# A list scheduler that counts VectorE's hold on GpSimd, first conversions ranked later, the guard moved into layer two, and a fourth silu buffer

## The chip, the cores and the metric

The kernel runs on one core of one Trainium2 chip. The metric is device microseconds of one execution, as the median of several runs. A core has a matrix engine (PE, TensorE), a vector engine (DVE, VectorE), an activation engine (ACT, ScalarE), a general engine (POOL, GpSimd), and a queue engine (SP, SyncE) that issues most of the DMAs. Each engine executes its own instructions strictly in the order in which they were written; engines wait for one another through semaphores.

## The reference, cut to what matters

A recurrent attention with 4 x 8 heads over 768 time steps, its output reshaped to 3072 tokens of 320 numbers, and then two dense layers on them:

```python
for t in range(S):                       # state: 40x40 for each of 32 heads
    y[:, :, t] = einsum('bhd,bhde->bhe', rt, state)
    Sa = einsum('bhde,bhe->bhd', state, at)
    state = state * wt[:, :, None, :] - einsum('bhd,bhe->bhde', Sa, bt) + einsum('bhd,bhe->bhde', vt, kt)
...
h = x @ w_in;  g = h * sigmoid(1.702 * h);  x = g @ w_out          # layer one, 320 -> 2048 -> 320
g = x @ w_gate;  x = (silu(g) * (x @ w_val)) @ w_out2              # layer two, 320 -> 1536 -> 320
```

The inputs are float32, but the weights of both layers arrive as float64, two 32-bit words to a number.

## The kernel before

**Attention.** The 768 time steps are cut into 12 pieces of 64 ("steps" from here on), which are solved one after the other for all heads at once. In a step VectorE scans the decays (L629, L648), k, b and a are scaled by them (L654 for kb, L658 for a, on VectorE or GpSimd), PE multiplies them (L680, L884), VectorE solves a triangular system in a long row of small products and updates (L760/L768 in the first five steps, L704/L712 later), PE and ScalarE join the parts (L802 to L854), and w, u, the state and y follow (L925 to L1100). Two steps give one block of 512 tokens, of which there are six.

**Layer one.** A block of 512 tokens goes through 16 slices of 128 hidden units: eight matmuls into the one PSUM bank h (L448), a silu on ScalarE into one of the buffers sg (L456), a high part gh (L462), a low part gl (L463), and eight matmuls into acc (L475 to L482) two slices later. After a block's sixteen slices three more sg buffers take its output (L494, L497, L504), from which DMAs write it to x2s in DRAM (L500, L508). There are three sg buffers; a silu waits until the DMA that reads its buffer has landed.

**Weights.** A weight piece (rows x 256 numbers) is loaded as float64 (L268, buffers cva) and turned into float32 by integer operations: L283 and L288 on VectorE, L280 on ScalarE, L296 on GpSimd. Beside it runs a guard, which finds numbers too small for this conversion. For the 44 pieces of layer one it is two ScalarE instructions (L271 squares, L274 compares and sums into flags); for the 45 pieces of layer two it is a minimum on VectorE (L299, into least). At the very end a flag is made of them (L1195 to L1206).

**What sets the order.** The attention and layer one are recorded as tasks with an engine (or two to choose from, VectorE or GpSimd), a cost and a due time, and a list scheduler (Plan.order) puts them into the order in which they are written. It knows that VectorE and GpSimd exclude each other (the variable port). Where it expects PE to be idle it writes filler matmuls on zeros (L408, tile still). Layer one's tasks have the last due time, so that they fill gaps of the attention. For tasks due before SOON, PE may wait up to 2 us for one that is due earlier. The tasks whose start is planned after the last attention task (the tail) are written one by one, with eleven small jobs of layer two's conversion after each slice. Layer two then runs in program order: for each of six blocks and twelve slices f sixteen matmuls (L1353), silu, product, high and low part (L1357 to L1360), and twelve matmuls of an earlier slice (L1372 to L1374).

Of the kernel before, what the change touches and what calls it, by code (L numbers as in the profile page):

```python
# [6 lines left out]
F32 = mybir.dt.float32  # L7
# [23 lines left out]
C_G = 192  # L31
# [40 lines left out]
class Plan:  # L72
# [6 lines left out]
    NEAR, SOON = {"PE": 2.0}, 2.5  # L79
# [40 lines left out]
    def order(self):  # L120
# [14 lines left out]
        def start(t, e):  # L135
# [90 lines left out]
class Convert:  # L226
# [4 lines left out]
    def __init__(self, tc, ctx, cst=None, flags=None):  # L231
        self.tc, self.nc = tc, tc.nc
        self.cst, self.flags = cst, flags
# [4 lines left out]
        self.count = self.parts = 0  # L238

# [7 lines left out]
    def piece(self, src, finish, least=None):  # L247
# [25 lines left out]
        def small():  # L273
            nc.scalar.activation(  # L274
                out=w, in_=w, func=ACTF.Relu, scale=-1.0, bias=self.cst[0:rows, C_G + 5:C_G + 6],
                accum_out=self.flags[0:rows, i:i + 1],
            )

# [19 lines left out]
        def smallest():  # L298
            v.tensor_reduce(  # L299
                out=least[0:rows], in_=hi.bitcast(F32), axis=AXL.X, op=ALU.min, apply_absolute_value=True  # L300
            )
# [7 lines left out]
        return [("SP", 0.5, load, (), (ak, ak + "l"), rows * cw / 128)] + check + [  # L309
            ("DVE", 0.25, shift, (ak,), (uk,), 0),  # L310
            ("DVE", 0.46, join, (ak,), (uk,), 0),
            guard,
            ("ACT", 0.44, low, (), (ak + "l",), 0),
            ("POOL", 0.78, add, (uk, ak + "l"), (wk,), 0),
        ] + finish(w)

# [26 lines left out]
class Up:  # L343
# [9 lines left out]
    def __init__(self, tc, ctx, keep, cst, w_out, x2s, side):  # L353
# [8 lines left out]
        self.sg = [k.tile([128, n], F32, name=f"sg{i}") for i in range(3)]  # L362
# [4 lines left out]
        self.still = k.tile([128, n], F32R, name="still")  # L367
# [38 lines left out]
    def warm(self):  # L406
        c = self.still
        self.nc.tensor.matmul(self.ph[0], c[:, 0:128], c, start=True, stop=True)  # L408

    def tasks(self, plan):  # L410
# [14 lines left out]
        def sg_slot():  # L425
            self.nsg += 1
            return (self.nsg - 1) % 3
# [763 lines left out]
def bad_flag(nc, tc, down, cst, flags, least, good, bad):  # L1191

    with tc.tile_pool(name="fl2", bufs=1, side="right") as p:
        m = p.tile([128, 1], F32, name="fl_f")
        nc.vector.tensor_reduce(out=m, in_=flags, axis=AXL.X, op=ALU.max)  # L1195
        nc.vector.tensor_scalar(out=m, in0=m, scalar1=0.0, scalar2=None, op0=ALU.is_le)
        nc.vector.tensor_tensor(m, m, good, op=ALU.mult)
        n = p.tile([128, 1], F32, name="fl_l")
        nc.vector.tensor_reduce(out=n, in_=least, axis=AXL.X, op=ALU.min)
        nc.vector.tensor_scalar(out=n, in0=n, scalar1=TINY, scalar2=None, op0=ALU.is_ge)  # L1200
        nc.vector.tensor_tensor(m, m, n, op=ALU.mult)
# [7 lines left out]
def layer_one(att, up, conv, jobs):  # L1209
# [26 lines left out]
class Down:  # L1236
# [5 lines left out]
    def __init__(self, tc, ctx, cst, conv, weights, x2s, out, up, least):  # L1242
# [8 lines left out]
        self.up, self.lag, self.n = up, [], 0  # L1251
        self.jobs = self.convert(conv, *weights)

# [5 lines left out]
    def convert(self, conv, gv, gv_rest, out, out_rest):  # L1259
# [46 lines left out]
        loads, makes, ends, n = [], [], [], 0  # L1306
        for f, src, fin in todo:
            got = []
            steps = conv.piece(src, lambda w: got.append(w) or [], self.least[:, n:n + 1])
            n += 1  # L1310
# [34 lines left out]
    def h_part(self, m, f):  # L1345
# [9 lines left out]
        sg, hi, lo = (t[self.n % 3] for t in (self.up.sg, self.up.gh, self.up.gl))  # L1355
# [28 lines left out]
    def prepare(self, n=0, f=-1):  # L1384

        while self.jobs and (n > 0 or self.jobs[0][0] <= f):
            self.jobs.pop(0)[1]()
            n -= 1
# [6 lines left out]
    def run(self):  # L1395
        for m in range(NSTEP):
            parts = iter(())
            for f in range(NF2):
# [9 lines left out]
                next(parts, None)  # L1408
                self.prepare(8)
# [7 lines left out]
def general(tc, cst, seq, w_in, w_out, w_gate, w_val, w_out2, xn, out):  # L1417
# [7 lines left out]
    with ExitStack() as ctx:  # L1425
# [64 lines left out]
        with ExitStack() as cx:  # L1490
            conv = Convert(tc, cx)

# [235 lines left out]
```

## Time and profile before

| | us |
|---|---|
| median of 3 runs (lowest to highest) | 1160.1 (1158.8 to 1166.8) |
| the profiled execution, its own time | 1152.7 |
| its span | 1150.9 |
| PE busy | 1103.5 (96%) |
| DVE busy | 683.8 (59%) |
| ACT busy | 474.6 (41%) |
| POOL busy | 165.1 (14%) |

The page says which engine carries the end: PE, with the fillers counted as busy. So the share of PE alone does not tell where time can go; the stretches, with the granted clock in each, and the waits of PE in them do. A filler is busy time that computes nothing, and a PE row at the lower clock takes twice as long as it has to.

### The profile page before, as it was taken

The page shows a single profiled execution, that of the slowest core. Times are in us where ns is not written, and L with a number is a line of the kernel's source. Part 1 is how long each engine was busy: PE and PEld are TensorE (multiplying, and loading weights), DVE is VectorE, ACT ScalarE, POOL GpSimd, SP SyncE. Part 2 cuts the span into 40 slices and gives each one's busy share as a digit, 9 for nine tenths or more (in the row PEclk, how much of TensorE's full clock was granted, in tenths as well). Part 3 has the DMA queues.
Part 4 walks back from the last instruction along what each step waited for, and adds up shares of the span by engine and source line. Part 5 has one row for each costly group of instructions (what it writes and reads, how often), then busy time and mean ns, then how long its engine had stood idle before and what let it go on. Part 6 is the DMA issues. An engine that isn't in the chain of part 4 may idle for free.

```text
span 1150.9 us, 39910 instructions
## 1 busy us (share of the span) xinstructions
PE 1103.5 (96%) x17425; PEld 914.1 (79%) x17425; DVE 683.8 (59%) x1400; ACT 474.6 (41%) x941; POOL 165.1 (14%) x144
## 2 busy tenths in 40 slices
PE   9888899989999999889999998999999999999996
PEld 7676777777887888768888786888888888888886
DVE  6856858686785959495876376878323232332222
ACT  3456577753434334333335355644222222222221
POOL 2222224250102002002110032322000000000000
PEclk9888999989999999998999999999999999999999
DMA  6245456553534444242423356733100101010000
GB/s 215 82 130 179 147 159 203 162 159 106 187 97 128 147 132 141 72 153 72 156 81 94 104 178 193 213 106 103 51 1 13 39 1 51 1 51 1 24 1 26
DMA packets 116440, 119.68 MB, mean 104 GB/s; under 512 B 13216, under 2 KB 107168, under 8 KB 116256
## 3 DMA queue, kind: packets, MB, share of 16 engines
q1 hardware_dynamic: 111288, 110.16, 31.4%
q10 hardware_dynamic: 4968, 6.88, 1.7%
q8 instruction: 138, 2.26, 0.8%
q14 instruction: 46, 0.38, 0.1%
HBM read 95.76 MB, written 13.11 MB: 95 GB/s over the span
## 4 chain that ended last, share of the span: by engine, by line
PE 84%; DVE 8%; issue 3%; DMA 2%; SPq 1%; ACT 1%; ACTq 0%; DVEq 0%
PE gv L1353 23%; PE h L448 14%; PE acc L480 4%; PE oacc L1374 4%; PE oacc L1373 4%; PE oacc L1372 4%; PE acc L482 3%; PE acc L481 3%; PE h L408 3%; PE ps L1120 2%; PE ps L1070 2%; PE ps L994 2%; PE acc L476 2%; PE acc L475 2%; DVE tmp L704 1%
## 5 line engine op out<-in xcount | busy, mean ns | idle before, releaser
L1353 PE MATMUL gv<-xst,wg 128*128 128x512 f32 x1152 | 274.4, 390 | 0.0
L1353 PEld LDWEIGHTS gv<-xst,wg 128*128 128x128 f32 x1152 | 213.5, 188 | 41.2
L448 PE MATMUL h<-xst,wi 120*128 120x512 f32 x768 | 202.0, 405 | 3.5 <-ACT sg L456 2.8
L448 PEld LDWEIGHTS h<-xst,wi 120*128 120x128 f32 x768 | 141.9, 190 | 37.5 <-ACT sg L456 3.4
L1358 DVE TENSOR_TENSOR sg<-gv,sg 128x512 f32<-128x512 f32 x72 | 49.7, 690 | 194.7 <-PE gv L1353 194.7
L456 ACT ACTIVATE sg<-h 128x512 f32<-128x512 f32 x96 | 57.2, 596 | 169.5 <-PE h L448 152.5
L296 POOL TENSOR_TENSOR cvw<-cvu,cva 128x256 uint32<-128x256 uint32 (+2 forms) x89 | 83.4, 938 | 264.9 <-DVE cvu L288 124.0
L463 DVE TENSOR_TENSOR gl<-sg,gh 128x512 fp32r<-128x512 f32 x81 | 59.0, 729 | 82.1 <-ACT gh L462 81.9
L1359 ACT ACTIVATE gh<-sg 128x512 fp32r<-128x512 f32 x72 | 45.5, 632 | 137.2 <-DVE sg L1358 137.2
L1357 ACT ACTIVATE sg<-gv 128x512 f32<-128x512 f32 x72 | 42.8, 595 | 128.5 <-PE gv L1353 128.5
L1374 PE MATMUL oacc<-wo,gl 128*128 128x320 f32 x288 | 89.0, 309 | 0.0
L1373 PE MATMUL oacc<-wo,gh 128*128 128x320 f32 x288 | 88.9, 309 | 0.0
L1372 PE MATMUL oacc<-wo,gh 128*128 128x320 f32 x288 | 88.6, 308 | 0.0
L408 PE MATMUL h<-still 128*128 128x512 f32 x254 | 77.5, 446 | 8.3 <-ACT sg L456 4.4
L480 PE MATMUL acc<-gh,wo 128*128 128x512 f32 x192 | 82.0, 427 | 0.6 <-DVE sg L497 0.6
L1360 DVE TENSOR_TENSOR gl<-sg,gh 128x512 fp32r<-128x512 f32 x72 | 49.8, 692 | 50.3 <-ACT gh L1359 50.3
L482 PE MATMUL acc<-gl,wo 128*128 128x512 f32 x192 | 76.5, 399 | 0.0
L481 PE MATMUL acc<-gh,wo 128*128 128x512 f32 x192 | 76.5, 398 | 0.0
L408 PEld LDWEIGHTS h<-still 128*128 128x128 f32 x254 | 50.4, 210 | 18.2 <-ACT sg L456 4.9
L462 ACT ACTIVATE gh<-sg 128x512 fp32r<-128x512 f32 x96 | 60.6, 632 | 3.1
L704 DVE TENSOR_TENSOR tmp<-tsol,nsol 128x126 f32<-128x126 f32 (+22 forms) x217 | 57.6, 266 | 6.8
L712 DVE TENSOR_TENSOR tsol<-tsol,tmp 128x126 f32<-128x126 f32 (+22 forms) x217 | 55.3, 255 | 6.8
(156 smaller groups left out, 1738.9 us busy)
## 6 DMA issues: line engine op xcount, KB each, us to landing
wo<-w_out SPq DMA_DIRECT2D x192, 160.0 KB
kb<-kba SPq DMA_DIRECT2D x96, 104.0 KB
cva<-out SPq DMA_DIRECT2D x64, 128.0 KB
cva<-gv SPq DMA_DIRECT2D x48, 128.0 KB
a<-kba SPq DMA_DIRECT2D x48, 104.0 KB
r<-rT SPq DMA_DIRECT2D x48, 104.0 KB
vt<-vT SPq DMA_DIRECT2D x48, 104.0 KB
w_out<-cvs SPq DMA_DIRECT2D x16, 256.0 KB
```

Source lines behind the costliest of these rows:

```text
L296: nc.gpsimd.tensor_tensor(w.bitcast(U32), u, lo, op=ALU.add)
L408: self.nc.tensor.matmul(self.ph[0], c[:, 0:128], c, start=True, stop=True)
L448: nc.tensor.matmul(ps[:, 0:n], self.wi[:, b, 128 * f:128 * f + 128], x[:, a], start=(e == 0), stop=(e == 7))
L462: add("ACT", 0.63, lambda: nc.scalar.activation(out=hi, in_=sg, func=ACTF.Copy), (f"sg{s}",), (f"gh{d}",))
L480: nc.tensor.matmul(acc[k], w[:, c:c + 128], hi, start=st, stop=False)
L481: nc.tensor.matmul(acc[k], w[:, 256 + c:384 + c], hi, start=False, stop=False)
L482: nc.tensor.matmul(acc[k], w[:, c:c + 128], lo, start=False, stop=sp)
L704: self.engine(e).tensor_tensor(tv, tsol[:, o:16, u:u + 1].to_broadcast([128, m, u]), nsol[:, u:u + 1, 0:u].to_broadcast([128, m, u]), op=A ...
L1353: nc.tensor.matmul(ps, w[:, b], x[:, a], start=(i == 0), stop=(i == 7))
L1372: nc.tensor.matmul(acc[k], hi[:, c], self.wo[:, f, 0], start=st, stop=False)
L1373: nc.tensor.matmul(acc[k], hi[:, c], self.wo[:, f, 1], start=False, stop=False)
L1374: nc.tensor.matmul(acc[k], lo[:, c], self.wo[:, f, 0], start=False, stop=sp)
```

## The change

Six edits:

1. In Plan.order, when a task may run on VectorE or on GpSimd, the start on the other engine is now taken not before the time at which the pair is free (busy = port).
2. SOON goes from 2.5 to 2.0.
3. The conversions of the first quarter of layer one's weights are due at 0.8 instead of 0.2, behind most of attention step one.
4. The guard is taken out of every conversion. In layer two, from the second block on, each of the 89 pieces is loaded a second time into cva, and VectorE takes its minimum into least; two pieces after each slice (look). The flag at the end is made of least alone.
5. Four sg buffers instead of three, in both layers.
6. The zeros of the filler are 128x128 instead of 128x512, read four times over by one matmul of the same size.

```diff
-    NEAR, SOON = {"PE": 2.0}, 2.5
+    NEAR, SOON = {"PE": 2.0}, 2.0
...
             for o, c in t.choice.items():
-                if o != e and max(t.est[o], free.get(o, 0.0)) + c < mine - 1e-9:
+                busy = port if t.port and o in ("DVE", "POOL") else 0.0
+                if o != e and max(t.est[o], free.get(o, 0.0), busy) + c < mine - 1e-9:
                     return None
...
-        guard = ("DVE", 0.47, zero, (wk,), (uk,), 0)
-        if self.flags is not None:
-            guard = ("ACT", 0.7, small, (), (wk,), 0)
-        check = [("ACT", 0.45, square, (ak,), (wk,), 0)]
-        if least is not None:
-            check, guard = [], ("DVE", 0.36, smallest, (ak,), (), 0)
...
+    def watch(self, src, least):
...
+        return [
+            ("SP", 0.5, load, (), (ak, ak + "l"), rows * cw / 128),
+            ("DVE", 0.36, self.smallest(a[0:rows, 0:cw, 1], least), (ak,), (), 0),
+        ]
...
-        self.sg = [k.tile([128, n], F32, name=f"sg{i}") for i in range(3)]
+        self.sg = [k.tile([128, n], F32, name=f"sg{i}") for i in range(4)]
...
-        self.still = k.tile([128, n], F32R, name="still")
+        self.still = k.tile([128, 128], F32R, name="still")
...
-                convert(jobs[q], 0.2 if q == 0 else 1.4 + 0.5 * q, 0.05)
+                convert(jobs[q], 0.8 if q == 0 else 1.4 + 0.5 * q, 0.05)
...
+    def look(self):
+        for t in self.seen:
+            t[1][2]()
+        self.seen = [self.looks.pop(0) for _ in range(min(2, len(self.looks)))]
+        for t in self.seen:
+            t[0][2]()
...
                 next(parts, None)
+                if m:
+                    self.look()
                 self.prepare(8)
```

In the order that results, 18 tasks go from GpSimd to VectorE (ten of them the scalings of a and kb, 104x1024), the fillers go from 254 to 231, and the first matmuls of layer one stand behind 209 fillers instead of 217. Ahead of the w product (L925, L939 in the change) of attention steps zero, one, two, three and eleven stand 90, 190, 217, 229 and 254 fillers before, and 108, 175, 211, 211 and 231 now; layer one's matmuls ahead of that of step eleven are 528 before and 576 now.

VectorE at the start, from the first scan of step zero on (c and rc are the scans, sv the scores, tmp and tsol the triangular solve). Before:

```order
L629 SCALAR_TENSOR_TENSOR c_131<-wdec,low 104x1040
L644 RECIPROCAL rc<-c_131 104x16
L648 SCALAR_TENSOR_TENSOR rc<-wdec,rc 104x1040
L654 TENSOR_TENSOR kb<-kb,rc 104x1024
L641 TENSOR_TENSOR ext<-ext,c_131 104x16
L654 TENSOR_TENSOR kb<-kb,rc 104x1024
L1126 TENSOR_TENSOR sv<-ps_125,cst 128x1024
L629 SCALAR_TENSOR_TENSOR c_132<-wdec,low 104x1040
L644 RECIPROCAL rc<-c_132 104x16
L648 SCALAR_TENSOR_TENSOR rc<-wdec,rc 104x1040
L736 STREAM_TRANSPOSE nsol<-nb_142 128x512
L887 TENSOR_TENSOR nk<-ps_125,cst 128x1024
```

And now:

```order
L643 SCALAR_TENSOR_TENSOR c_130<-wdec,low 104x1040
L658 RECIPROCAL rc<-c_130 104x16
L662 SCALAR_TENSOR_TENSOR rc<-wdec,rc 104x1040
L672 TENSOR_TENSOR a_127<-a_127,c_130 104x1024
L668 TENSOR_TENSOR kb<-kb,rc 104x1024
L655 TENSOR_TENSOR ext<-ext,c_130 104x16
L668 TENSOR_TENSOR kb<-kb,rc 104x1024
L750 STREAM_TRANSPOSE nsol<-nb_141 128x512
L643 SCALAR_TENSOR_TENSOR c_131<-wdec,low 104x1040
L759 SCALAR_TENSOR_TENSOR nsol<-nsol,cst 128x16x16
L774 TENSOR_TENSOR tmp<-tsol,nsol 128x15
L782 TENSOR_TENSOR tsol<-tsol,tmp 128x15
```

The scaling of a for step zero has come from GpSimd, and the transpose that opens step zero's solve has moved ahead of step one's two scans and of sv.

PE between the nk product of step zero and the nb product of step one. Before:

```order
L408 MATMUL h<-still 128x512 x21
L925 MATMUL ps_126<-v,nk 64x40 x32
L408 MATMUL h<-still 128x512 x36
L802 MATMUL ps_125<-cst 128x512
L808 MATMUL ps_125<-nsol,tsol 16x32 x64
L408 MATMUL h<-still 128x512 x4
```

And now:

```order
L420 MATMUL h<-still 128x512 x43
L939 MATMUL ps_125<-v,nk 64x40 x32
L420 MATMUL h<-still 128x512 x5
L816 MATMUL ps_124<-cst 128x512
L822 MATMUL ps_124<-nsol,tsol 16x32 x64
L420 MATMUL h<-still 128x512 x10
```

The 36 fillers that PE spent on step zero's solve are 5 now, and the 21 ahead of the w product are 43.

VectorE in layer two, two slices of the second block. Before:

```order
L1358 TENSOR_TENSOR sg_97<-gv,sg_97 128x512
L1360 TENSOR_TENSOR gl_103<-sg_97,gh_100 128x512
L1358 TENSOR_TENSOR sg_98<-gv,sg_98 128x512
L1360 TENSOR_TENSOR gl_104<-sg_98,gh_101 128x512
L1358 TENSOR_TENSOR sg_99<-gv,sg_99 128x512
```

And now:

```order
L1371 TENSOR_TENSOR sg_98<-gv,sg_98 128x512
L1373 TENSOR_TENSOR gl_104<-sg_98,gh_101 128x512
L306 TENSOR_REDUCE least<-cva_77 120x1
L306 TENSOR_REDUCE least<-cva_78 120x1
L1371 TENSOR_TENSOR sg_95<-gv,sg_95 128x512
```

Two minima stand behind each slice's low part; each reads a piece whose load was issued one slice earlier.

## Rows read from the trace of the kernel before

**Rows 1.** The page: busy time, share of the span and instructions of each engine.

```profile
PE 1103.5 (96%) x17425; PEld 914.1 (79%) x17425; DVE 683.8 (59%) x1400; ACT 474.6 (41%) x941; POOL 165.1 (14%) x144
```

**Rows 2.** Stretches: PE, PEld, DVE, ACT, POOL busy; PEclk, DMA share, GB/s.

```profile
0.00:50.00 50.00, 45.26 (x743) 35.87 (x747) 38.65 (x71) 18.75 (x39) 13.06 (x14) 0.97 0.50 155
50.00:100.00 50.00, 43.52 (x1295) 34.82 (x1287) 35.23 (x75) 29.55 (x76) 14.29 (x18) 0.83 0.48 148
100.00:150.00 50.00, 44.02 (x1502) 34.91 (x1495) 35.92 (x73) 30.86 (x67) 10.58 (x11) 0.97 0.50 157
...
500.00:550.00 50.00, 45.31 (x1073) 36.44 (x1072) 35.99 (x79) 18.99 (x31) 6.92 (x4) 0.90 0.38 115
...
700.00:750.00 50.00, 50.00 (x214) 40.19 (x215) 38.64 (x86) 30.64 (x67) 15.51 (x16) 1.00 0.64 187
...
850.00:900.00 50.00, 50.00 (x263) 44.17 (x262) 15.80 (x24) 13.70 (x24) 0.00 (x0) 1.00 0.09 30
```

**Rows 3.** Timeline of PE, start-up: start, length, instruction, idle time before and its releaser.

```profile
1.64 15.64 PE L408 MATMUL h<-still 128*128 128x512 f32 x59 [1.64 <-DVE still L368]
...
32.58 8.46 PE L408 MATMUL h<-still 128*128 128x512 f32 x36
...
53.81 0.58 PE L408 MATMUL h<-still 128*128 128x512 f32 x1 [2.15 <-issue]
54.32 1.99 PE L884 MATMUL ps<-a,kb 40*64 40x64 f32 x64
...
116.27 1.16 PE L884 MATMUL ps<-a,kb 40*64 40x64 f32 x64 [0.49 <-DVE mt L1026]
...
139.78 2.13 PE L448 MATMUL h<-xst,wi 120*128 120x512 f32 x8
```

**Rows 4.** Timeline of POOL (first row) and DVE, step zero's scalings.

```profile
9.04 3.61 POOL L658 TENSOR_TENSOR a<-a,c 104x1024 f32<-104x1024 f32 x1 [6.78 <-DMA a<-kba]
...
10.70 3.03 DVE L654 TENSOR_TENSOR kb<-kb,rc 104x1024 f32<-104x1024 f32 x1
...
13.76 1.21 DVE L654 TENSOR_TENSOR kb<-kb,rc 104x1024 f32<-104x1024 f32 x1
```

**Rows 5.** Lines by source: count, then shortest, median and longest in ns.

```profile
L658 POOL TENSOR_TENSOR a<-a,c x7: 2181/2202/4212, 9.0 to 576.3; 104x1024 f32<-104x1024 f32 x7
...
L658 DVE TENSOR_TENSOR a<-a,c x5: 1183/1219/2627, 89.5 to 420.8; 104x1024 f32<-104x1024 f32 x5
...
L274 ACT ACTIVATE cvw<-cvw,cst x44: 492/509/512, 25.0 to 250.4; 128x256 f32<-128x256 f32 x20, 120x256 f32<-120x256 f32 x16, 80x256 f32<-80x256 f32 x8
...
L299 DVE TENSOR_REDUCE least<-cva x45: 403/412/416, 660.5 to 798.4; 128x1 f32<-128x256 f32 x45
```

**Rows 6.** Waits of PE, 450 to 550 us: us in total, times, longest.

```profile
PE h L408 <- ACT sg L456: 4.4, 1, 4.4
PE ps L845 <- DVE nk L887: 3.2, 1, 3.2
```

**Rows 7.** Timeline of PE behind the 4.4 us wait.

```profile
517.69 1.96 PE L408 MATMUL h<-still 128*128 128x512 f32 x4 [4.43 <-ACT sg L456]
519.58 1.92 PE L845 MATMUL ps<-tt,nb 32*32 32x32 f32 x64
```

**Rows 8.** Timeline, end of a block of layer one: last output, next silu, next matmuls.

```profile
695.05 0.35 ACTq L500 DMA_DIRECT2D x2s<-sg  x1
...
699.35 0.60 ACT L456 ACTIVATE sg<-h 128x512 f32<-128x512 f32 x1 [4.80 <-DMA x2s<-sg]
...
700.00 2.13 PE L448 MATMUL h<-xst,wi 120*128 120x512 f32 x8 [2.79 <-ACT sg L456]
```

**Rows 9.** Timeline, the flag at the end: first and third instruction of it, and PE's.

```profile
1142.36 0.24 DVE L1195 TENSOR_REDUCE fl_f<-flags 128x1 f32<-128x96 f32 x1
...
1142.83 0.16 DVE L1197 TENSOR_TENSOR fl_f<-fl_f,good 128x1 f32<-128x1 f32 x1
...
1143.54 0.27 PE L1203 MATMUL gv<-cst,fl_f 128*1 128x128 f32 x1 [1.62 <-DVE fl_f L1201]
```

More of the change, by code (lines that the diff above doesn't have):

```diff
@@ L238, in __init__ @@
         self.count = self.parts = 0
+        self.flush = False
     def engine(self, e):
@@ L296, in add @@
             nc.gpsimd.tensor_tensor(w.bitcast(U32), u, lo, op=ALU.add)
[L298 to L301, printed above, removed]
[L303 to L309 removed]
+        first, guard = [], []
+        if self.flush:
+            first = [("ACT", 0.45, square, (ak,), (wk,), 0)]
+            guard = [("DVE", 0.47, zero, (wk,), (uk,), 0)]
+        return [("SP", 0.5, load, (), (ak, ak + "l"), rows * cw / 128)] + first + [
             ("DVE", 0.25, shift, (ak,), (uk,), 0),
             ("DVE", 0.46, join, (ak,), (uk,), 0),
[L312 removed]
+        ] + guard + [
             ("ACT", 0.44, low, (), (ak + "l",), 0),
@@ L315, in piece, with smallest, load @@
         ] + finish(w)
+    def smallest(self, hi, least):
+        return lambda: self.nc.vector.tensor_reduce(
+            out=least[0:hi.shape[0]], in_=hi.bitcast(F32), axis=AXL.X, op=ALU.min, apply_absolute_value=True
+        )
+    def watch(self, src, least):
+        if src.dtype == F32:
+            return []
+        rows, cw = src.shape[0], src.shape[1] // 2
+        i = self.count % 3
+        self.count += 1
+        a, ak = self.a[i], f"cva{i}"
+        def load():
+            to = a[0:rows, 0:cw].rearrange("p c k -> p (c k)")
+            for c in (slice(0, cw), slice(cw, 2 * cw)):
+                self.nc.sync.dma_start(out=to[:, c], in_=src[:, c])
+        return [
+            ("SP", 0.5, load, (), (ak, ak + "l"), rows * cw / 128),
+            ("DVE", 0.36, self.smallest(a[0:rows, 0:cw, 1], least), (ak,), (), 0),
+        ]
     def wkey(self):
@@ L1240, with __init__ @@
     LAG = 2
-    def __init__(self, tc, ctx, cst, conv, weights, x2s, out, up, least):
+    def __init__(self, tc, ctx, cst, conv, weights, first, x2s, out, up, least):
         self.least = least
@@ L1305, in convert @@
                 todo.append((f, out_rest[i // 2], lambda w, i=i: second_rest(w, i // 2)))
-        loads, makes, ends, n = [], [], [], 0
+        self.raw = [src for _, src, _ in todo]
+        loads, makes, ends = [], [], []
         for f, src, fin in todo:
             got = []
-            steps = conv.piece(src, lambda w: got.append(w) or [], self.least[:, n:n + 1])
-            n += 1
+            steps = conv.piece(src, lambda w: got.append(w) or [])
             loads.append(steps[0][2])
@@ L1384, in prepare @@
     def prepare(self, n=0, f=-1):
-        while self.jobs and (n > 0 or self.jobs[0][0] <= f):
+        need = [i + 1 for i, job in enumerate(self.jobs) if job[0] <= f]
+        for _ in range(min(len(self.jobs), max(need + [n]))):
             self.jobs.pop(0)[1]()
-            n -= 1
+    def look(self):
[4 more added lines that the diff above has]
+            t[0][2]()
     def begin(self):
@@ L1617, in build @@
                     weights = [words(t) for t in (gv, gv_rest, out2, out2_rest)]
-                    down = Down(tc, down_ctx, cst, conv, weights, x2s, out, up, least)
+                    first = [words(t)[i] for t in (in_ab, in_m) for i in range(t.shape[0])]
+                    first += [words(out1)[q, i] for q in range(4) for i in range(5)]
+                    down = Down(tc, down_ctx, cst, conv, weights, first, x2s, out, up, least)
                     left = sum(t.eng == "PE" for t in tail)
```

40 lines of the change are left out of this document (17 added, 23 removed).

## The prediction, made before the result was known

> **What bounds the kernel now.** The first view is the page: PE is busy 1103.5 of 1150.9 us [rows 1]. That count takes the 254 fillers for work, and rows at the lower clock for full ones, so the next view is the one by stretches [rows 2]. From 700 us on PE is busy for all of a stretch at full clock: whatever the other engines gain or lose there is hidden as long as PE's operands come in time. In the first 150 us it is different. PE is idle for 4.7, 6.5 and 6.0 us of the three stretches (50 less 45.26, 43.52, 44.02), and the granted clock is 0.97, 0.83, 0.97. The clock has two levels, 1.0 and 0.5 of 2.4 GHz, so a mean of 0.83 is 17 of 50 us at 1.2 GHz, and 8.5 us lost; the other two lose 1.5 us each. The timeline of PE shows what lies in between: 59 fillers from 1.64 to 17.28 us, 36 more from 32.58 us (8.46 us, 0.235 us each), and layer one's first matmul only at 139.78 us [rows 3]. So the start-up is a chain of VectorE, PE and ScalarE in which PE fills time; behind it PE is nearly the bound, with a few waits. Of these the longest that another engine causes are 4.4 and 3.2 us between 450 and 550 us, both for a late solve on VectorE (the 4.4 us are named after a silu, which stood behind a copy of that solve's result on ScalarE) [rows 6], and 2.8 us at the end of a block [rows 8].
>
> The profiled execution took 1152.7 us, 7.4 us less than the median of the runs shown. The sum below is made against 1152.7 and then taken off 1160.1.
>
> **The change, part by part.**
>
> *VectorE instead of GpSimd, and the fillers.* In the profile the two engines stand in each other's way: kb's scaling took 3.03 us while GpSimd scaled a (3.61 us), and 1.21 us by itself [rows 4]. The ten large scalings that move cost 1.22 us each on VectorE and 2.20 on GpSimd at the median [rows 5]. Were each pair serial, a move would give back 0.98 us of both engines' time, 9.8 us for ten; but only what stands in front of a waiting PE counts. The order shows how the scheduler turned this into fillers: step zero's solve begins before step one's scans, 36 fillers beside it become 5, the 21 ahead of it 43, and in all 23 fewer are left, 8 before layer one's first matmul and 15 behind it. At 0.235 us [rows 3] that is 23 x 0.235 = **5.4 us**. The bounds: nothing, if PE now waits where it filled; and 9.8 us, if all moved work stood in the path. I take 5.4, because the real matmuls are the same on both sides, and a filler that isn't there can only come back as a wait.
>
> Here a rule of the Trainium skill speaks against the change. The rows first: after a wait of 2.15 us the next product (L884) took 1.99 us, where the same product took 1.16 us after a wait of 0.49 us [rows 3]. The page "TensorE: Matmul & The Clock Gate", section "HAM oscillation — how this bites in real kernels", says that an array which waits between groups of matmuls falls back to half rate and begins the next group cold. By that rule fewer fillers mean more waits and more half rate, and the 5.4 us would be lost again; the trace agrees as far as a wait stands before the slow rows, and shows no case of fillers alone being missed. It is the first rival below.
>
> *SOON and the due time of the first conversions* only change which task goes first. The first conversions stand in the middle of step one on VectorE as before, and layer one's first matmul comes earlier in the order, so no price is added: 0, bounded by one product late or early, 1.2 us [rows 3].
>
> *The guard out of layer one's conversions* takes 44 squares and 44 comparisons off ScalarE, the latter 0.51 us each, 22 us in all [rows 5], between 25 and 250 us, where ScalarE is busy 19 to 31 of 50 us [rows 2]. No wait of PE in the rows is for them. I take 0, since PE's other operands hide it; if a copy of PE's result stands behind one comparison, 0.5 us each in a dozen places, 6 us, is the other end.
>
> *The guard out of layer two's conversions*: 45 minima of 0.41 us, 18.5 us of VectorE between 660 and 798 us [rows 5], where PE is busy 50.00 of 50 [rows 2]: 0.
>
> *The minima in layer two's blocks.* 89 x 0.41 = 36.7 us of VectorE. A slice is 28 matmuls, and PE does 263 of them in a stretch of 50 us [rows 2], so a slice lasts 5.3 us and VectorE is busy 1.7 us of it; two minima make that 2.5 us. The matmuls that need a low part come two slices later, about 10 us, against 0.82 us of delay. The loads: 178 DMAs, about 22 MB, in 45 slices or 240 us, some 90 GB/s more in stretches that move 30 GB/s; the start-up moves 155 [rows 2]. Each load has a slice's time to land. So 0, and the cover is PE; without it, 45 slices x 0.82 = 37 us is the far end. The output DMAs of a block stand behind such loads on SP, but the last block has no loads any more.
>
> *Four silu buffers.* Three outputs of a block fill the three buffers; the next silu began at 699.35 us, 4.3 us after the last output DMA was issued (695.05), and PE's next matmuls lost 2.79 us [rows 8]. With a fourth buffer that silu writes a free one; the second after it needs the DMA's buffer, a slice later, when it has landed. **2.8 us**, with 0 and 2.8 as its bounds; the other blocks show no such wait of PE, so once.
>
> *The flag at the end.* PE waits 1.62 us for it, and six small VectorE instructions run from 1142.36 to 1143.54 us, on the path [rows 9]. Three go: half of 1.18, **0.6 us**.
>
> *The smaller filler tile* clears a quarter as much; the first filler waited 1.64 us for it [rows 3], but step zero's chain doesn't: 0.
>
> *The late solves.* Both waits of rows 6 come from steps whose share of layer one is small: VectorE has too little time beside PE's. The order now spreads layer one's matmuls more evenly (576 ahead of step eleven's w product instead of 528). Bounds 0 and 4.4 + 3.2 = 7.6 us, with the clock behind them another 5 us (0.90 in the stretch from 500 us is 10 us at the lower level, and four fillers took 1.96 us there [rows 2, 7]). Nothing in the trace says which it is; I take half of the waits, **3.8 us**, and none of the clock.
>
> The sum is 5.4 + 2.8 + 0.6 + 3.8 = 12.6 us: a profiled execution like this one would take 1140.1 us, and the median 1160.1 - 12.6 = **1147.5 us**, or 1143 to 1153 for this case by itself.
>
> **The rivals.**
>
> *The fillers come back as waits.* For it: PE's idle time in the start-up is already 17 us although fillers were meant to cover it, and waits bring the lower clock. Against it: step zero's solve really begins earlier in VectorE's order. Only the silu buffer and the flag are left: 2.8 + 0.6, 1156.7 us. Chance 0.23.
>
> *The late solves vanish with their clock.* All of 7.6 and 5 us instead of 3.8: 12.6 + 3.8 + 5 = 21.4, 1138.7 us. For it: the more even spread; against it: VectorE takes over ten scalings. Chance 0.18.
>
> *Slower: PE starves on its own instructions.* Waits that end at "issue" are for nothing that the profile shows, and they stand where PE runs many small products (1295 matmuls between 50 and 100 us, against 214 in a stretch of layer one alone [rows 2]). Fewer fillers put such products closer together. A stretch that behaves like 50 to 100 us instead of 100 to 150 us loses 0.5 us more in idle time and 7 us more in clock. From two more such stretches (15 us) the gain is used up; three give 22.5 - 12.6 = 10 us, 1170 us. Against it: the sequences of small products are those of before, in another place. Chance 0.10.
>
> *The minima hold layer two back*, if a load takes longer than a slice on SP, so that VectorE waits in front of the next product. Half a microsecond per slice is 22 us, 1160.1 - 12.6 + 22 = 1170 us; it decides once a low part is late by more than the two slices of slack. Chance 0.04.
>
> **How the numbers follow.** The forecast keeps 0.45. The range runs from a little under the second rival, 1136, to above the first, 1164, which also holds the ends of the unpriced terms; the two slower rivals and some tail, 0.2, stay outside. About 1% is what a measurement of this kernel can tell from no change (its own runs spread 0.7%), 11.6 us, so faster is below 1148.5. A bit over half of the forecast's cases lie there, 0.26, with the second rival 0.18, and 0.01 for the rest: 0.45. Slower, above 1171.7, is half or more of the last two, 0.09; the rest, 0.46, is within 1%.
>
> **What would show it.** Fillers: L448's counterpart begins near 135 us or before, and PE's idle time in the first 150 us is not above 17 us; if it is, the first rival holds. Silu buffer: no wait of PE behind the outputs of a block in the tail. Solves: the largest wait of PE between 300 and 650 us is below 4 us. Minima: PE busy 50 of 50 us in layer two with VectorE near 23. A stretch at 0.83 behind 150 us would show the third rival, and PE below 49.5 in layer two the fourth. The forecast is wrong if layer two's first matmul doesn't come some 12 us earlier.

## The result, and the profile of the change

The change took 1145.9 us (median of four executions, 1142.0 to 1149.2) and the kernel before, on the same chip, 1161.3 us (1158.8 to 1166.8). The ratio is 0.986, with an interval of 0.981 to 0.991: a gain of 1.4%. The forecast of 1147.5 us was 1.6 us too high. Its sum came out; whether its terms did is a second question, and the answer is mixed. One more execution of the change, in the run that repeats it, took 2075.8 us for a reason that is not known, and no number here is made from it.

The page of the change, busy time of each engine, answers to [rows 1]:

```profile
PE 1091.8 (96%) x17402; PEld 907.4 (80%) x17402; DVE 697.1 (61%) x1459; ACT 437.8 (38%) x809; POOL 112.5 (10%) x125
```

The span fell from 1150.9 to 1140.2 us, by 10.7, and PE's busy time by 11.7. PE waited as long as before: adding up its waits by releaser gives 37.0 us before and 37.4 now. So the gain is busy time of PE, not waiting. The matmuls other than fillers are 17171 on both sides. The fillers' time fell by 8.5 us (their rows are shown further down), and that of the other matmuls, at the same count, by the remaining 3.2.

The stretches, columns as in [rows 2]:

```profile
0.00:50.00 50.00, 46.33 (x855) 36.78 (x856) 38.08 (x71) 14.78 (x27) 7.17 (x11) 0.98 0.52 154
50.00:100.00 50.00, 44.42 (x1363) 35.59 (x1362) 36.31 (x76) 22.72 (x48) 11.23 (x16) 0.88 0.49 147
100.00:150.00 50.00, 42.44 (x1175) 33.76 (x1173) 36.05 (x73) 20.88 (x41) 8.52 (x10) 0.83 0.50 151
...
500.00:550.00 50.00, 48.02 (x1104) 38.77 (x1102) 36.06 (x81) 19.84 (x33) 2.60 (x2) 1.00 0.44 134
...
700.00:750.00 50.00, 49.84 (x217) 40.19 (x216) 34.02 (x70) 28.99 (x65) 12.23 (x16) 1.00 0.67 192
...
850.00:900.00 50.00, 50.00 (x262) 44.12 (x261) 21.70 (x42) 13.40 (x24) 0.00 (x0) 1.00 0.32 99
```

PE's idle time in the first 150 us is 16.8 us (3.67 + 5.58 + 7.56) against 17.2 in [rows 2]. The clock there is no better: a mean of 0.98, 0.88 and 0.83 where it was 0.97, 0.83 and 0.97. Between 500 and 550 us the idle time fell from 4.7 to 2.0 us and the clock rose from 0.90 to 1.00. In layer two (last row) PE is busy in all of the stretch, with 5.9 us more of VectorE and three times the DMA traffic beside it, at no cost.

PE's start-up, which answers to [rows 3]:

```profile
1.18 17.34 PE L420 MATMUL h<-still 128*128 128x512 f32 x63 [1.18 <-DVE still L380]
...
24.85 10.04 PE L420 MATMUL h<-still 128*128 128x512 f32 x43
...
36.12 1.42 PE L420 MATMUL h<-still 128*128 128x512 f32 x5
...
131.49 2.00 PE L462 MATMUL h<-xst,wi 120*128 120x512 f32 x8
```

Layer one's first matmul comes at 131.49 instead of 139.78 us. Step zero on VectorE, whose scalings answer to [rows 4]; the third row is the transpose that opens step zero's solve:

```profile
10.45 1.20 DVE L672 TENSOR_TENSOR a<-a,c 104x1024 f32<-104x1024 f32 x1
11.56 1.22 DVE L668 TENSOR_TENSOR kb<-kb,rc 104x1024 f32<-104x1024 f32 x1
...
21.01 1.10 DVE L750 STREAM_TRANSPOSE nsol<-nb 128x512 f32<-128x512 f32 x1 [6.99 <-ACT nb L602]
```

The scaling of a, 3.61 us on GpSimd with kb's stretched to 3.03 us beside it, is 1.20 us on VectorE and kb's 1.22. The transpose began at 29.20 us before and begins at 21.01 now.

PE's waits from 300 to 650 us; [rows 6] show the two of 4.4 and 3.2 us that stood there:

```profile
PE ps L1084 <- issue: 4.3, 3, 2.5
PE ps L898 <- ACT tok L602: 3.2, 4, 1.6
PE ps L694 <- issue: 1.0, 2, 0.9
PE ps L859 <- DVE nk L901: 0.2, 1, 0.2
```

The late solves are gone (L859, the same line as L845 before, waits 0.2 us), but other waits stand there: 8.7 us in all, where it was 9.1 (7.6 for the late solves and 1.5 for "issue").

The end of a block in layer one's tail, which answers to [rows 8]:

```profile
685.81 0.44 ACT L275 ACTIVATE cva<-cva 128x256 uint32<-128x256 uint32 x1 [2.90 <-DMA cva<-gv]
...
686.49 0.68 DVE L511 TENSOR_SCALAR sg<-acc 128x512 f32<-128x512 f32 x1
...
687.23 0.50 PE L494 MATMUL acc<-gh,wo 128*128 128x512 f32 x1 [2.58 <-DVE sg L511]
```

The silu no longer waits for a buffer. But ScalarE stood 2.90 us, and VectorE 1.82 us, on a piece of layer two's weights (cva) that had not landed, and the block's outputs (L508 on ScalarE, L511 on VectorE) stood behind it on both engines: PE now waits 2.58 us for L511, where it waited 2.79 us for the silu. The flag, which answers to [rows 9]:

```profile
1131.85 0.24 DVE L1209 TENSOR_REDUCE fl_f<-least 128x1 f32<-128x96 f32 x1
...
1132.53 0.27 PE L1213 MATMUL gv<-cst,fl_f 128*1 128x128 f32 x1 [1.13 <-DVE fl_f L1211]
```

### The profile page after: what moved, and what is told of

Read it like the earlier page. It is cut to its first block, busy times and chain, and to the rows that moved or that the text cites. A ratio compares the mean times of both kernels' runs of the same rounds, so it can differ in the third digit from the quotient of the medians.

```text
span 1140.2 us, 39997 instructions
## 1 busy us (share of the span) xinstructions
PE 1091.8 (96%) x17402; PEld 907.4 (80%) x17402; DVE 697.1 (61%) x1459; ACT 437.8 (38%) x809; POOL 112.5 (10%) x125
## 4 chain that ended last, share of the span: by engine, by line
PE 87%; DVE 4%; DMA 3%; issue 3%; ACT 1%; SPq 1%; ACTq 0%; DVEq 0%
PE gv L1366 23%; PE h L462 16%; PE acc L494 4%; PE h L420 4%; PE oacc L1387 4%; PE oacc L1386 4%; PE oacc L1385 4%; PE acc L495 3%; PE acc L496 3%; PE ps L1084 2%; PE ps L1008 2%; PE ps L1134 2%; PE acc L490 2%; PE acc L489 2%; PE ps L694 2%
## 5 line engine op out<-in xcount | busy, mean ns | idle before, releaser
L291 POOL TENSOR_TENSOR cvw<-cvu,cva 128x256 uint32<-128x256 uint32 (+2 forms) x89 | 71.2, 801 | 242.5 <-DVE cvu L283 110.4
L420 PE MATMUL h<-still 128*128 128x512 f32 x231 | 69.0, 445 | 1.9 <-DVE still L380 1.2
L726 DVE TENSOR_TENSOR tsol<-tsol,tmp 128x126 f32<-128x126 f32 (+22 forms) x217 | 58.2, 268 | 6.7
L477 POOL TENSOR_TENSOR gl<-sg,gh 128x512 fp32r<-128x512 f32 x15 | 22.5, 1501 | 392.1 <-ACT gh L476 349.8
```

The lines of the kernel that those rows point to most:

```text
L291: nc.gpsimd.tensor_tensor(w.bitcast(U32), u, lo, op=ALU.add)
L420: self.nc.tensor.matmul(self.ph[0].rearrange("q (k c) -> q k c", k=4), c, c.unsqueeze(1).to_broadcast([128, 4, 128]), start=True, stop=True)
L477: add(("DVE", "POOL"), (0.74, 1.35), lambda e: self.engine(e).tensor_tensor(lo, sg, hi.bitcast(F32), op=ALU.subtract), (f"sg{s}", f"gh{d}" ...
```

## The experiments

Each experiment is one kernel; its ratio is to the kernel before, run beside it, with a 95% interval. "Change less X" is the change with X undone, "before with X" the kernel before with X alone. The last column is the time of the one execution that the kernel's profile shows; it can lie well off the median.

| kernel | ratio | interval | median us | fillers | profiled us |
|---|---|---|---|---|---|
| the change | 0.986 | 0.981 to 0.991 | 1145.9 | 231 | 1142.0 |
| before, again | 1.002 | 1.000 to 1.005 | 1164.0 | 254 | 1162.3 |
| change less edit 1 | 0.981 | 0.977 to 0.985 | 1142.0 | 246 | 1148.6 |
| change less the fourth sg buffer | 0.996 | 0.992 to 0.999 | 1160.0 | 232 | 1149.8 |
| change with SOON at 2.5 | 0.997 | 0.994 to 1.000 | 1159.1 | 253 | 1154.2 |
| change without the guard | 0.983 | 0.979 to 0.986 | 1143.9 | 231 | 1149.6 |
| change less edit 4 (old guard) | 0.987 | 0.982 to 0.992 | 1147.7 | 248 | 1147.8 |
| before with edit 4 | 0.980 | 0.976 to 0.984 | 1139.3 | 232 | 1146.5 |
| before with edits 5 and 6 | 1.000 | 0.997 to 1.003 | 1163.7 | 259 | 1166.1 |
| before with edit 1 | 0.997 | 0.994 to 1.001 | 1158.6 | 252 | 1161.3 |
| change less edit 1, nine jobs | 0.980 | 0.974 to 0.985 | 1138.4 | 246 | 1144.4 |
| before with edit 4, nine jobs | 0.990 | 0.987 to 0.993 | 1147.6 | 232 | 1142.8 |

**Edit 1 undone.**

```diff
-                busy = port if t.port and o in ("DVE", "POOL") else 0.0
-                if o != e and max(t.est[o], free.get(o, 0.0), busy) + c < mine - 1e-9:
+                if o != e and max(t.est[o], free.get(o, 0.0)) + c < mine - 1e-9:
```

> The change with its first edit undone: the scheduler again compares VectorE with GpSimd without the time at which the pair is free. The order has 246 fillers (231 in the change), 214 of them ahead of layer one's first matmul (209). Theory 'fillers' (each filler more is 0.235 us): 15 x 0.235 = 3.5 us longer than the change, 1149 to 1150. Theory 'GpSimd's hold' (the large scalings back on GpSimd cost about 1 us each on the path): 8 to 12 us longer, 1154 to 1158. Theory 'guard' (the gain comes from the guard's instructions that left ScalarE in the start-up): within 2 us of the change.

0.981 (0.977 to 0.985): without its first edit the change is not slower; whether it is a little faster, the overlapping intervals don't tell. Fifteen of the 23 fillers are back (246), and the time is not. So the fillers that edit 1 takes away are not the cause of the gain.

**Three sg buffers.** The change with range(3) and % 3 again.

```diff
-        self.sg = [k.tile([128, n], F32, name=f"sg{i}") for i in range(4)]
+        self.sg = [k.tile([128, n], F32, name=f"sg{i}") for i in range(3)]
...
-            return (self.nsg - 1) % 4
+            return (self.nsg - 1) % 3
...
```

> The change with three silu buffers again, in both layers. 232 fillers (231). My prediction's step: the wait behind a block's outputs in the tail comes back and costs 2.8 us, 1148.7. Rival: the outputs of that block are themselves late in the change's profile (PE waits 2.6 us for one), so the silu's wait lies beside that one and the time stays within 1 us of the change.

0.996 (0.992 to 0.999): the fourth buffer is worth about 1% within the change, 11 us, not 2.8. Where it goes is not at the end of a block, but in the middle of layer one. PE's largest waits in this kernel:

```profile
PE ps L859 <- DVE nk L901: 7.3, 3, 3.0
```

And one of the three in PE's timeline:

```profile
406.71 0.40 PE L489 MATMUL acc<-gh,wo 128*128 128x512 f32 x1
410.09 1.92 PE L859 MATMUL ps<-tt,nb 32*32 32x32 f32 x64 [2.99 <-DVE nk L901]
411.94 3.78 PE L462 MATMUL h<-xst,wi 120*128 120x512 f32 x8
```

With three buffers the scheduler orders differently and the late solves are back, with the lower clock behind this one: the granted clock is 0.50 from 411.9 to 415.7 us, and eight matmuls take 3.78 us there, 2.00 us in the start-up of the change. So the late solves go with the buffer here. The profile is of the shortest of twelve executions (1149.8 us, the median is 1160.0). It shows 7.3 us of such waits and does not show 11.

**SOON at 2.5.**

```diff
-    NEAR, SOON = {"PE": 2.0}, 2.0
+    NEAR, SOON = {"PE": 2.0}, 2.5
```

> The change with SOON at 2.5 again. 253 fillers (231), all 22 of the difference behind layer one's first matmul. Theory 'fillers': 22 x 0.235 = 5.2 us longer, 1151. Theory 'start-up' (the gain is made ahead of layer one's first matmul, and fillers behind it stand beside waits that exist anyway): within 2 us of the change. My prediction priced SOON at nothing, apart from what it does to fillers.

0.997 (0.994 to 1.000): SOON, priced at nothing, is worth 1% within the change. PE's largest waits in its profile:

```profile
PE ps L939 <- issue: 8.5, 5, 2.8
PE ps L694 <- issue: 8.5, 8, 1.8
PE h L462 <- ACT sg L470: 4.6, 3, 1.9
```

Waits for "issue" (nothing that the profile shows) in front of the small products of the attention steps are 8.5 us each on two lines; the longest sums in the change are 5.5 and 5.1 us. All waits for "issue" add up to 24.9 us here, 19.6 and 20.7 in the two profiles of the change. That these waits are the 1% is not shown: edit 1 alone, below, has only 13.5 us of them and gains nothing. The fillers are 253, nearly the 254 of before.

**No second look.** The change with the call of look taken out; it leaves out the guard of layers one and two altogether.

```diff
-                if m:
-                    self.look()
```

> The change without the loads and minima in layer two: the guard on the weights is left out altogether. My prediction's step (they lie under PE, price 0): within 1 us of the change, PE busy 50 of 50 us in layer two in both. Rival (they hold layer two back): shorter by 3 us or more.

0.983 (0.979 to 0.986) against the change's 0.986 (0.981 to 0.991): the 178 loads and 89 minima in layer two cost nothing that can be told apart here, as forecast.

**The old guard in the change.** All edits but edit 4: squares and comparisons (small) on ScalarE in layer one's conversions, minima in layer two's, the old flag.

```diff
+        guard = ("DVE", 0.47, zero, (wk,), (uk,), 0)
+        if self.flags is not None:
+            guard = ("ACT", 0.7, small, (), (wk,), 0)
+        check = [("ACT", 0.45, square, (ak,), (wk,), 0)]
+        if least is not None:
+            check, guard = [], ("DVE", 0.36, smallest, (ak,), (), 0)
...
-                if m:
-                    self.look()
```

> The change with the guard where it was: two ScalarE instructions per piece in the start-up, a minimum on VectorE in layer two's conversions, no second loads. 248 fillers (231 in the change). Theory 'guard' (ScalarE, freed of 88 instructions, lets the start-up run faster: layer one's first matmul came 8 to 12 us earlier in the change and in all four kernels with one part undone): about 8 us longer than the change, 1152 to 1156, and layer one's first matmul back near 138 us. Theory 'order' (the start-up's gain is that step zero's solve begins earlier, by the due time and the scheduler's comparison): within 3 us of the change, first matmul at 132 us or before. My prediction priced this part at 0, with 6 us as its end.

0.987 (0.982 to 0.992): the other edits together give the whole gain without edit 4. Layer one's first matmul comes at 127.8 us, so the earlier start doesn't need the guard's move.

**The guard's move alone.** The same difference, the other way round, applied to the kernel before.

> The kernel before with the guard moved to layer two as the only edit. 232 fillers (254 before). Theory 'fillers': 22 x 0.235 = 5.2 us shorter than before. Theory 'guard': 6 to 10 us shorter, layer one's first matmul near 131 us. Theory 'order': within 3 us of before, first matmul near 139 us.

0.980 (0.976 to 0.984): edit 4 alone gives at least as much as the whole change, 22 us, and takes the fillers to 232. This is the largest part, and the prediction had it at 0. Layer one's first matmul comes at 134.4 us, between the two that were expected. The profile is of the longest of six executions (1146.5 us), so it doesn't show where a usual one gains the rest. With the run before it: either edit 4 or the other edits do it, and both together do no more. The parts don't add.

**Four sg buffers and the small filler tile alone.** Before, with edits 5 and 6.

```diff
-        self.sg = [k.tile([128, n], F32, name=f"sg{i}") for i in range(3)]
+        self.sg = [k.tile([128, n], F32, name=f"sg{i}") for i in range(4)]
...
-        self.still = k.tile([128, n], F32R, name="still")
+        self.still = k.tile([128, 128], F32R, name="still")
...
```

> The kernel before with four silu buffers in both layers, and the small filler tile that makes room for the fourth. 259 fillers (254 before). My prediction's step: 2.8 us shorter than before. Theory 'buffers' (three buffers stop layer one for some 5 us at every block's end, PE takes the attention's tasks closer together, and then waits for the solve on VectorE; undoing this part cost 14 us): 8 to 14 us shorter, and no wait of PE for the solve above 2 us between 400 and 550 us. Theory 'fillers': 1 us longer.

1.000 (0.997 to 1.003). As a whole the two edits give nothing by themselves. Its profile has a wait in layer two that neither kernel has, here in PE's waits:

```profile
PE gv L1355 <- DMA wg<-wg: 9.5, 1, 9.5
```

PE stands still for a piece of layer two's weights. The jobs that convert them are done at eleven for each slice of layer one that is left after the last attention task. The order leaves 20 slices here, so 220 of the 396 jobs are done in the tail, against 24 slices and 264 jobs in the kernel before. The profiles agree: the step on GpSimd that each of the 45 pieces takes (L296 in the kernel before) has begun for 24 pieces here, and for 29 before, when layer two's first matmul begins. Where the scheduler moves layer one forward, the conversions lose slices. No run has the four buffers alone with more jobs a slice, so what they would give without these 9.5 us stays open.

**Nine jobs in the tail, without edit 1.**

```diff
-                            down.prepare(11)
+                            down.prepare(9)
```

> The change with its first edit undone and with nine jobs of layer two's conversion after each slice of the tail instead of eleven. A piece has 7.7 jobs now instead of 8.7, so eleven jobs take pieces faster than their loads land; in the change's profile ScalarE and VectorE wait 2.9 us for one ahead of a block's output, and PE 2.6 us for that. Theory: that wait goes, 2 to 3 us shorter than the kernel with the first edit undone, 1139 to 1140. Rival (the load was late for another reason, or the wait lies beside others): within 1 us of it.

0.980 (0.974 to 0.985), the lowest median, 1138.4 us. PE's waits from 660 to 740 us, all of them:

```profile
PE acc L493 <- DVE sg L510: 0.3, 1, 0.3
```

The wait at the end of the block is gone, and with it those for the silu: the same order with eleven jobs has 3.0 us of waits in its tail. Without the guard a piece takes 7.8 jobs where it took 8.8 (351 instead of 396 jobs for the same 45 pieces; the expectation has 7.7 and 8.7), so eleven jobs a slice ask for a load sooner than before, and ScalarE reaches a piece that has not landed. Nine come nearer to the old pace: 1.15 pieces a slice (9 / 7.8) against 1.25 before and 1.41 in the change. The order leaves 24 slices here, so 216 of 351 jobs are done in time. The gain over eleven jobs (0.981) is inside the intervals, so the median can't show what the profile does.

**Nine jobs with the guard's move alone.** The same line in the kernel with edit 4 alone.

> The kernel before with the guard moved to layer two, and nine conversion jobs after each slice of the tail instead of eleven; nothing else. The guard alone took 0.980 of before. Its profile has 4.8 us of waits of PE in the tail, 2.7 us for a silu and 2.1 us for a block's output. Theory 'loads' (eleven jobs take pieces faster than they land, and the outputs stand behind them): the 2.1 us go and the silu's wait for its buffer stays, about 2 us shorter than the guard alone, 0.978 of before, 1137. Rival: the outputs' wait only uncovers the silu's, 0.980.

0.990 (0.987 to 0.993), slower than with eleven (0.980). The order leaves 20 slices, nine jobs a slice make 180 of 351, and the wait for late weights is back:

```profile
783.93 0.31 PE L1384 MATMUL oacc<-wo,gl 128*128 128x320 f32 x1
784.08 0.63 PE L1363 MATMUL gv<-xst,wg 128*128 128x512 f32 x2
791.79 1.62 PE L1363 MATMUL gv<-xst,wg 128*128 128x512 f32 x3 [7.09 <-DMA wg<-wg]
```

That is 7.09 us, and the two medians differ by 8.3. The two profiles can't confirm that the wait is the difference, since the one with the wait is the shorter (1142.8 against 1146.5 us). With eleven jobs the same order does 220 of 351 and has no such wait. Counted by the step on GpSimd, the profiles with 24 pieces (four buffers alone) and 22 pieces (here) begun before layer two's first matmul wait for weights, and all others, with 27 or more, don't.

**Edit 1 alone.** The two lines of edit 1 in the kernel before.

> The kernel before with the first edit as the only one: the scheduler's comparison counts the time at which VectorE and GpSimd are free. 252 fillers (254 before), 212 of them ahead of layer one's first matmul (217). My prediction's step gave this edit most of the fillers' 5.4 us and part of the solves' 3.8: 5 to 9 us shorter than before. Theory 'guard and due time' (undoing the edit in the change cost nothing, 0.981 of before against 0.986): within 3 us of before, though layer one's first matmul may come some us earlier than at 139.8 us.

0.997 (0.994 to 1.001): nothing that can be told from no change. Its stretches are cut at layer one's first matmul and at layer two's first:

```profile
0.00:130.50 130.50, 119.93 (x2973) 96.66 (x2974) 94.14 (x195) 66.79 (x155) 25.02 (x30) 0.86 0.51 153
130.50:757.30 626.80, 602.53 (x12420) 479.83 (x12419) 457.22 (x1004) 297.50 (x590) 78.42 (x78) 0.96 0.46 140
```

Edit 1 does what it says: the transpose that opens step zero's solve begins at 20.5 us here, and in every profile with edit 1 between 19.8 and 21.1; without it between 28.6 and 29.9. Layer one's first matmul comes at 130.5 us, and yet layer two's only at 757.3. A start 9 us earlier is lost again over the next 600 us, which have a mean clock of 0.96; what loses it is not shown.

**Both kernels again, unchanged**, for a second profile of each.

> The kernel before, unchanged, for a second profiled execution: the first took 1152.7 us, below every one of the 40 other executions of it beside my experiments (1157.9 to 1175.4, median near 1162), so it doesn't show where a usual one loses another 9 us. Theory 'late weights': a usual execution waits in layer two's first block for the copy of weights (wg), as the kernel with four buffers alone did for 9.5 us behind 800 us. Theory 'supply': the same waits as in the first profile, only more of those that end at issue and more time at the lower clock, in the attention.

> The change, unchanged, for a second profiled execution beside the kernel before of the same call. Its first took 1142.0 us, the lowest of its four executions. Theory 'late weights': PE 50 of 50 us through layer two again, since the guard's 45 minima no longer stand in the conversions, and the whole difference to a usual execution of before above 11 us lies in layer two's first block. Theory 'supply': layer two is the same in both, and the difference lies ahead of its first matmul.

Before took 1162.3 us in this profile and the change 1147.1, a difference of 15.2 us, as between the medians; the first pair differs by 10.7, since both were short executions, before's by more: 1152.7 us is below every other execution of it on record, and 1142.0 is the lowest of the change's four. The stretches of before, cut as above:

```profile
0.00:139.80 139.80, 125.17 (x3235) 98.93 (x3235) 104.45 (x206) 69.82 (x162) 36.64 (x39) 0.89 0.49 149
139.80:758.30 618.50, 590.91 (x12165) 472.42 (x12158) 436.16 (x946) 293.25 (x574) 112.77 (x90) 0.98 0.46 138
```

And of the change:

```profile
0.00:126.10 126.10, 112.00 (x2969) 90.14 (x2970) 93.18 (x194) 50.49 (x100) 23.85 (x33) 0.93 0.54 161
126.10:743.90 617.80, 589.31 (x12402) 473.08 (x12402) 434.87 (x942) 272.56 (x498) 75.66 (x75) 0.97 0.46 138
```

The start-up is 13.7 us shorter, the middle the same. In the first pair the start-up is 8.3 us shorter (139.8 to 131.5) and the middle 2.1. PE's idle time in the start-up is 14.6 us before and 14.1 now, so 13.2 of the 13.7 us are busy time: eight fillers and 258 other matmuls fewer (3235 to 2969 in all), most of the others small products of step two that now stand behind layer one's first matmul, and a better clock, 0.89 to 0.93. The first pair has no better clock in the start-up (0.91 and 0.90). The middle has those small products in addition, and 15 fillers fewer. PE's waits of before, 300 to 650 us, in this second profile:

```profile
PE h L408 <- ACT sg L456: 4.4, 1, 4.4
PE ps L845 <- DVE nk L887: 3.1, 1, 3.1
PE ps L680 <- issue: 2.1, 5, 0.7
PE acc L475 <- DVE sg L506: 0.4, 1, 0.4
```

And of the change:

```profile
PE ps L1084 <- issue: 4.1, 3, 2.1
PE ps L898 <- ACT tok L602: 2.9, 4, 1.4
PE ps L694 <- issue: 1.1, 2, 0.7
...
```

The late solves belong to before's order, and the waits that stand there instead to the change's: both are there in both profiles, 10.0 us in all before and 10.1 now, with four shorter waits that are left out above. Over the whole execution PE's waits add up to 40.4 us before and 40.1 now.

## Why the prediction was right, and where it was not

**The sum** was 12.6 us, and the medians differ by 15.4. As to causes, one small term stands (the flag), one is right in its sign and wrong in its origin (the fillers), and two were made up for elsewhere (the buffer and the late solves). That the total came within 1.6 us is in good part luck: the 6.6 us that were forecast for those two brought nothing in the sum of PE's waits (37.0 to 37.4 us, 40.4 to 40.1), and PE's busy time fell by 11.7 and 14.9 us where 5.4 was put down for it.

**Fillers (5.4 us).** Mechanism half right, size low, cause wrong. Fillers are 23 fewer, and they did not come back as waits. These lines show the size. Before, first and second profile:

```profile
L408 PE MATMUL h<-still 128*128 128x512 f32 x254 | 77.5, 446 | 8.3 <-ACT sg L456 4.4 <-issue 2.1 <-DVE still L368 1.6
...
L408 PE MATMUL h<-still 128*128 128x512 f32 x254 | 77.8, 445 | 8.6 <-ACT sg L456 4.4
```

And the change:

```profile
L420 PE MATMUL h<-still 128*128 128x512 f32 x231 | 69.0, 445 | 1.9 <-DVE still L380 1.2 <-ACT sg L470 0.7
...
L420 PE MATMUL h<-still 128*128 128x512 f32 x231 | 66.0, 430 | 1.9 <-DVE still L380 1.2
```

The fillers' time fell by 8.5 us, in the second pair by 11.8. A filler took 0.31 us on the mean before (77.5 / 254), not the 0.235 of a row at full clock: some stand at the lower clock (four took 1.96 us in [rows 7]) and some alone (one took 0.58 us in [rows 3]). Of the 10.7 and 15.2 us between the spans that is most; the other matmuls, as many as before, took 3.2 and 3.1 us less, which the prediction has no term for. But the step said that edit 1 takes them away, and edit 1 alone takes 2 of them (252), the guard's move alone 22 (232). And fillers are no measure of the time: 232 of them go with 0.996 (three buffers) and with 0.980 (edit 4 alone), 246 with the lowest median. They come with the scheduler's order; their number does not set the time.

**SOON (0)** was mis-priced: undone, it costs about 1%. An edit that "only changes which task goes first" had been bounded by one product late, 1.2 us. It changed more than which of two tasks goes first: with SOON at 2.5 the order has 22 fillers more, all behind layer one's first matmul. Neither SOON nor the due time was tried by itself in the kernel before.

**The guard out of layer one's conversions (0, far end 6)** is the step that failed most, with 22 us by itself. The work it removes was under-counted too: the start-up's 20 comparisons (L274) have 19 READ_ACCUMULATOR instructions of 0.19 us behind them, which the prediction did not see. ScalarE's busy time in the start-up falls from 69.8 to 52.7 us with edit 4 alone, and over the whole execution by 36 to 38 us, against 474.6 and 476.0 in the two profiles of before. The argument for 0 was that no wait of PE is put down to ScalarE's comparisons. But a kernel whose order is planned with these tasks in it does not only lose them: the plan is made again, with 232 fillers instead of 254 and 20 slices in the tail instead of 24. How much of the 22 us is the new order and how much the freed ScalarE is not shown.

**Guard and minima in layer two (0)** hold: 0.983 without the second look, and PE busy in 50.00 of 50 us.

**Four sg buffers (2.8).** The wait that it was to remove was removed, and 2.58 us of another came in its place. Edit 4 has a part in it, with fewer jobs for each piece and the same jobs for each slice: with the old guard in the change this wait is 0.82 us. The order has a part as well, since the change less edit 1, also with eleven jobs, has 0.72. The prediction had no rival for that. (Its issue at 695.05 us is not the last of the block's outputs, as it says; L508's follows at 695.64. The 2.79 us don't depend on that.) In the change the fourth buffer is worth 1% all the same, not at a block's end but, as far as its profile shows, by the late solves that stay away in the middle of layer one.

**The flag (0.6)**: PE waits 1.13 instead of 1.62 us, 0.5 us. Right.

**The late solves (3.8)**: they are gone in both profiles, 7.6 and 7.5 us down to 0.2 and 0.6, and the wait time in that stretch is the same (9.1 to 8.7, 10.0 to 10.1). So the term brought nothing by the way that was forecast. The waits came back as "issue" and as copies of ScalarE. What stayed is the clock: in the stretch from 500 us it rose from 0.90 to 1.00, in the second pair from 0.90 to 0.97.

**The rivals.** The first, that fillers come back as waits, did not happen: with fewer fillers PE's waits stayed the same in sum. The clock does fall behind some waits, as in the 3.78 us at 0.50 behind 2.99 us of waiting, above, but not behind all: in the change a product behind a wait of 1.60 us, at 505.84 us, took 1.16 us, as at full clock. The Trainium skill, "TensorE: Matmul & The Clock Gate", section "HAM oscillation — how this bites in real kernels", says that waiting between groups brings half rate; the row behind 2.99 us agrees, and no run here shows fillers alone being missed. The second, late solves gone with their clock, happened in part. The third, waits for "issue", is not seen in the change: 17.3 us before and 19.6 now in the first pair, 22.6 and 20.7 in the second. With SOON at 2.5 there are 24.9. The fourth did not come.

**What was to be seen**: layer one's first matmul by 135 us (131.5 and 126.1), the largest wait between 300 and 650 us below 4 (2.5), layer two's first matmul 12 us earlier (10.4 and 14.4), VectorE near 23 in layer two (21.7): all as foretold. Idle time in the first 150 us not above 17: 16.8 in the first profile and 17.3 in the second, where before's second has 15.0. By that sign alone the first rival would hold in the second pair, and yet PE's waits in sum did not grow, so this sign does not tell the two apart. No wait behind the outputs of a block: not so. The 100 to 150 us stretch has 0.83, but no stretch of 50 us from there to 700 us is below 0.97 in the first profile of the change or below 0.90 in the second.

**What stays open.** Why these orders differ by one to two per cent beyond the waits named, and why edit 4 alone gives as much as all edits, isn't settled. Two profiles of one kernel differ by nearly ten microseconds in the middle (609.0 and 618.5 for the same order), which is as much as what is to be explained, and the profile of edit 4 alone is of its longest execution. The two variants with the lowest medians, edit 4 alone (0.980) and the change less edit 1 with nine jobs (0.980), lie below the change, but their intervals overlap with its own.

## What to carry to other kernels

Where a scheduler writes the order, price no edit by the work it removes or by "nothing waits for it": run each edit alone and each undone, and judge by medians, since one profile can be off by as much as the gain. After work is taken out of a stream that is handed out in so many jobs per slice, count again how many jobs a piece takes and how many slices are left. A reduced wait is a gain only once the sum of waits in its stretch has fallen.

## What the runs showed of the hardware

Two things were not expected. A comparison with a running sum on ScalarE (L274) is followed by a separate READ_ACCUMULATOR of 0.19 us, over a third on top of its 0.51 us; in the kernel before:

```profile
L274 ACT ACTIVATE cvw<-cvw,cst 128x256 f32<-128x256 f32 (+2 forms) x44 | 22.3, 506 | 1.1
...
L274 ACT ACTIVATION_READ_ACCUMULATOR cvw<-cvw,cst 128x1 f32 (+2 forms) x44 | 8.2, 187 | 0.0
```

And the same kernel, unchanged, spent 609.0 and 618.5 us in the same middle stretch of some 12,160 matmuls, with PE's waits for "issue" between 140 and 300 us at 5.4 and 10.7 us: waits for nothing that the profile shows differ between two executions by 5.3 us, close to half of the whole forecast gain.
